# The exponentials of an attention kernel: shift read from a per-key bias instead of added by VectorE, and the range test's branch moved to the end

## The chip, the cores and the metric

The kernel runs on one core of a Trainium2 chip. The core has five engines that each run their own list of instructions in order and wait for one another through semaphores: TensorE (PE; its weight loads are shown as PEld), VectorE (DVE), ScalarE (ACT), GpSimd (POOL) and SyncE (SP, here the main issuer of DMAs). Matmul results land in PSUM, everything else is in SBUF or DRAM. The metric is device time in microseconds (us) for one execution. The kernel before takes 1242.67 us, the median of three runs (1242.14 to 1245.28).

## The reference

Two blocks, one after the other. First a causal attention whose scores get a decay bias; then a mixture of experts in which each token goes to one expert.

```python
# B, H, S, DH = 8, 8, 576, 64;  q, k = randn * 0.1;  s = randn * 0.5
scores = scale * q @ k.T                      # scale = 1/8
cum = np.cumsum(np.maximum(s, 0.0), axis=-1)
bias = -(cum[:, :, :, None] - cum[:, :, None, :])
scores = np.where(causal, -1000000000.0, scores + np.minimum(bias, 0.0))
attn = np.exp(scores - np.max(scores, axis=-1, keepdims=True))
attn = attn / (np.sum(attn, axis=-1, keepdims=True) + 1e-09)
x = attn @ v                                  # then the heads side by side: (B, S, 512)
...
logits = x @ w_gate;  local_gate = sigmoid(x @ w_local)       # 8 experts
# per batch, token after token: e = argmax(logits) at s == 0 or local_gate < 0.5,
# else the expert of the token before
out = softmax(logits)[e] * (np.maximum(x @ w1[e], 0.0) @ w2[e])   # w1: 512x1024
```

A key j after its query i is masked. For the others the bias is cum[j] - cum[i], which is never above 0, so the minimum changes nothing. Dividing by the sum takes out any factor that is the same for all keys of a query; a shift of cum by a constant is such a factor.

## The kernel before

**Stages.** attention, in_range, route, a branch, experts. `manual_schedule` means that each engine gets its instructions in the order in which the code writes them; nothing reorders them, and waits are put in where data or a buffer asks for it.

**Attention.** The 64 heads go in 32 pairs (NPAIR; HP = 4 pairs a batch, index n); the two heads of a pair lie in the two halves of the partitions of qb and kb. Scores are made key by key: the partitions are 128 keys of block c, the columns are the queries from that block on, so block 0 has 576 columns a head, then 448, 320, 192, and the last 64 keys ("tail") 64. `scores(n, c)` issues the matmuls into PSUM (L207 for block 0, L212 for blocks 1 to 3, L220 for the tail, whose 64x64 results go into free columns of the PSUM tile of block 3). VectorE then adds the bias in one pass for each head (L230, L221 for the tail): it adds cb, the cumulated sums of the queries, spread over all partitions, and subtracts ck, the value of each key, a number for each partition, and so moves the scores to SBUF. POOL masks the diagonal 128x128 squares (L232, L224), and ScalarE takes the exponential of the whole tile with both heads in SBUF (L234, L226).

`values(n, t)` multiplies with the values: query block t = 0 to 3 (L251, one matmul of 74 columns for each key block up to t and each head, with the exponentials as weights) and the tail queries (L263, and L267 for the tail keys). The 74 columns of va are the 64 of a head's v, its 9 logit columns (v times the gate weights), and a column of ones that gives the sum of the exponentials. VectorE takes reciprocals of the sums into recs (L255, L269) and scales the results (L257, L270, L271). The 9 logit columns are made once a batch by `value_logits(b)`: matmuls (L179) into PSUM, two ScalarE copies to SBUF (L181, L182), PE transposes (L185), ScalarE copies into va and vl (L187, L190).

The order within an iteration n is written in the loop at L294: scores blocks 0, 1 of pair n; values 0, 1, 2 of pair n - 1; scores blocks 2, 3 and tail of pair n; values 3 and tail of pair n - 1. After the fourth pair of a batch comes value_logits of the next one; one pair later the batch before is stored (L310, L312, the DRAM buffer x_tokens) and its logits are summed (`logits`, VectorE L280 and L283, then PE L285, into lg).

The PSUM pool ps_s has three buffers of two banks, tag "s": block 0 takes one for each head, blocks 1, 2 and 3 one for both heads, the tail shares that of block 3, and value_logits takes one for L179 and one for L185. ps_o has two buffers for values and for L285.

**Loads.** SP loads q, k, vT and v of batch b + 1 at the second pair of batch b (L118 to L123). cum is computed on VectorE before the first pair, written to DRAM, and read back spread over the partitions: cb for each pair (`load_cum`, 32 times), cbt for the tails, ctail for ck.

**After attention.** `in_range` counts on VectorE how many reciprocals in recs lie outside SUM_MIN to SUM_MAX (0.25 to 1e18), into out_of. `route` turns lg into the experts of the tokens: lists of tokens idx_g and idx_s in 43 blocks (NBLK) of 128 tokens, the expert ebi of each block and the gate. Then all engines read out_of (L76) and branch (L78): if it is over 0, attention_general computes attention again with a true maximum, and route runs again. Then `experts`, for each block: w1 and w2 of its expert are loaded by SP (L765, 2 MB each), its tokens are gathered by POOL (L773), transposed on PE (L782), two layers (L794, relu on ScalarE L795, transposes L803, L810), VectorE scales (L812), POOL scatters the rows to the output (L813).

The first weight load of the experts writes SBUF that attention and route used, so it waits for them too.

## Time and profile before

One profiled execution:

| | |
|---|---|
| profiled execution, own time | 1241.2 us |
| its span, first to last instruction | 1239.5 us |
| busy PE / PEld / DVE / ACT / POOL | 1105.6 / 653.4 / 337.4 / 198.9 / 163.6 us |
| granted TensorE clock, mean | 0.86 of full |
| attention ends (last L285) | 518.5 us |
| route and branch | 518.5 to 568.7 us |
| experts, from the first transpose of tokens | 577.8 us to the end |
| DMA | 269.44 MB, mean 217 GB/s |

How to read the rows that follow. On the page's slices the span is cut into 40 equal parts of 31 us, and a digit is the busy share of an engine there in tenths; PEclk is the TensorE clock that was granted, in tenths of full speed. In rows of groups or of the timeline, "L251 PE MATMUL po<-va,sc 128*128 128x74" is an operation of line 251 on PE that writes po from va and sc; "[1.50 <-DVE sc L230]" says that the engine stood still 1.50 us ahead of it, until the DVE operation of L230 was done. In rows of the waits, the operation that waited stands first and the one that ended the wait second. In rows of windows the start and end are followed by the length, and busy us and number of instructions of each engine, then the granted clock, the share of the 16 DMA engines and GB/s.

### The profile page before, as it was taken

Reading aid. Unit: us, or ns where it says so; the run is one execution under the profiler, and the core shown is the slowest. Engines: PE = TensorE matmul, PEld = TensorE weight load, DVE = VectorE, ACT = ScalarE, POOL = GpSimd, SP = SyncE. Lnnn points to the kernel's source line nnn. Section 1 sums busy time; section 2 is a strip of 40 time slices with the busy share of each in tenths; the row PEclk is TensorE's granted clock in tenths of the full one; section 3 lists DMA queues with packets and bytes.
Section 4 is the critical chain, followed back from the end, with each engine's and each line's share of the span. In section 5 each row is a group of like instructions: output and inputs, shape, how many; then the busy total and the mean of one; then the engine's idle time right before and its main releaser. Section 6 shows DMA issues by size and latency. Waiting matters only on the chain. (4 is left out here: it accounts for less than half of the span.)

```text
span 1239.5 us, 12883 instructions
## 1 busy us (share of the span) xinstructions
PE 1105.6 (89%) x4870; PEld 653.4 (53%) x4870; DVE 337.4 (27%) x799; ACT 198.9 (16%) x332; POOL 163.6 (13%) x306
## 2 busy tenths in 40 slices
PE   2889898989898989745999999999999999999996
PEld 1666666666576666643444445444444444444443
DVE  1544443434444444460111111111111111111110
ACT  1322222222222222100111111111111111111110
POOL 0111111111111111121011111111111111111110
PEclk9777777777767777655999999999999999999998
DMA  8616161616251611106978887878878888777860
GB/s 247 217 53 216 54 214 56 213 56 212 77 191 45 224 47 31 39 1 253 409 305 308 311 318 309 316 308 316 323 308 319 319 313 317 308 305 297 307 227 4
DMA packets 47959, 269.44 MB, mean 217 GB/s; under 512 B 18381, under 2 KB 18381, under 8 KB 33808
## 3 DMA queue, kind: packets, MB, share of 16 engines
q1 hardware_dynamic: 39920, 247.79, 54.0%
q0 software_dynamic: 6880, 20.72, 4.2%
q8 instruction: 41, 0.67, 0.2%
q10 hardware_dynamic: 1088, 0.02, 0.1%
q14 instruction: 30, 0.25, 0.1%
HBM read 249.48 MB, written 20.86 MB: 218 GB/s over the span
## 5 line engine op out<-in xcount | busy, mean ns | idle before, releaser
L794 PE MATMUL hp<-w1b,xT 128*128 128x512 f32 x688 | 311.8, 597 | 0.8 <-DVE xT L784 0.8
L810 PE MATMUL yp<-w2b,hT 128*128 128x512 f32 x688 | 302.4, 593 | 0.3 <-ACT hT L804 0.3
L810 PEld LDWEIGHTS yp<-w2b,hT 128*128 128x128 f32 x688 | 130.9, 190 | 164.3 <-issue 163.8
L794 PEld LDWEIGHTS hp<-w1b,xT 128*128 128x128 f32 x688 | 128.4, 192 | 146.0 <-issue 144.9
L251 PEld LDWEIGHTS po<-va,sc 128*128 128x128 f32 x1280 | 179.8, 226 | 36.2 <-issue 33.9
L251 PE MATMUL po<-va,sc 128*128 128x74 f32 x1280 | 191.0, 315 | 0.0
L230 DVE SCALAR_TENSOR_TENSOR sc<-cb,ck,ps 128x576 f32<-128x576 f32 (+3 forms) x256 | 141.5, 609 | 135.0 <-issue 62.7
L234 ACT ACTIVATE sc<-sc 128x1152 f32<-128x1152 f32 (+3 forms) x128 | 105.0, 843 | 299.6 <-POOL sc L232 299.1
L795 ACT ACTIVATE hs<-hp 128x512 f32<-128x512 f32 x86 | 51.4, 597 | 615.9 <-PE hp L794 615.9
L812 DVE TENSOR_SCALAR y<-yp,gate 128x512 f32<-128x512 f32 x43 | 32.3, 751 | 401.6 <-PE yp L810 401.6
L813 POOL DMA_INDIRECT out_dram<-y,idx_s x43 | 43.6, 1015 | 564.2 <-DVE y L812 564.2
L232 POOL TENSOR_SCALAR_AFFINE_SELECT sc<-sc 128x256 f32<-128x256 f32 x128 | 51.8, 406 | 422.8 <-DVE sc L230 408.5
L212 PE MATMUL ps<-qb,kb 64*128 64x320 f32 (+2 forms) x384 | 88.0, 569 | 0.0
L207 PE MATMUL ps<-qb,kb 64*128 64x512 f32 (+1 forms) x256 | 74.5, 731 | 0.0
L804 DVE COPY hT<-htp 128x512 f32<-128x512 f32 x43 | 29.7, 691 | 155.2 <-PE htp L803 151.6
L207 PEld LDWEIGHTS ps<-qb,kb 64*128 64x128 f32 x256 | 36.9, 312 | 36.8 <-issue 35.9
L220 PE MATMUL ps<-qb,kb 64*64 64x64 f32 x128 | 10.8, 246 | 48.3 <-DVE sc L230 48.3
L803 PEld LDWEIGHTS htp<-ident,hs 128*128 128x128 f32 x344 | 40.3, 141 | 22.6 <-issue 22.6
L773 POOL DMA_INDIRECT xg<-x_tokens,idx_g x43 | 42.0, 978 | 21.8 <-issue 12.8
L803 PE MATMUL htp<-ident,hs 128*128 128x128 f32 x344 | 44.6, 273 | 0.0
L212 PEld LDWEIGHTS ps<-qb,kb 64*128 64x128 f32 x384 | 39.4, 233 | 8.4 <-DVE sc L230 1.1
L263 PE MATMUL pot<-va,sc 128*64 128x74 f32 x512 | 40.1, 336 | 0.0
(129 smaller groups left out, 426.8 us busy)
## 6 DMA issues: line engine op xcount, KB each, us to landing
w1b<-in_w_dram SPq DMA_DIRECT2D x43, 2048.0 KB, 13.5
w2b<-in_w_dram SPq DMA_DIRECT2D x43, 2048.0 KB, 8.5
cb<-cum SPq DMA_DIRECT2D x32, 576.0 KB, 4.6
qb<-in_q_dram SPq DMA_DIRECT2D x8, 1152.0 KB, 6.1
kb<-in_k_dram SPq DMA_DIRECT2D x8, 1152.0 KB, 8.2
vTb<-in_vT_dram SPq DMA_DIRECT2D x8, 1152.0 KB, 10.7
va<-in_vm_dram SPq DMA_DIRECT2D x8, 1024.0 KB, 15.4
x_tokens<-xb SPq DMA_DIRECT2D x8, 1024.0 KB, 4.3
```

The costliest lines, as they stand in the source:

```text
L207: mm(ps[h][:, a:z], lhsT=kb[d, hp, :P], rhs=qb[d, hp, a:z], start=True, stop=True)
L212: mm(both[:, h, :w], lhsT=kb[d, hp, c * P : c * P + P], rhs=qb[d, hp, c * P :], start=True, stop=True)
L230: nc.vector.scalar_tensor_tensor(sc[:, h], cb[:, h, c * P :], ck[:, i : i + 1], ps[h], Alu.subtract, Alu.add)
L232: nc.gpsimd.affine_select(out=diag, in_=diag, compare_op=Alu.is_ge, fill=MASKED / scale, base=0, pattern=[[0, 2], [1, P]], channel_multipl ...
L234: nc.scalar.activation(sc, sc, Act.Exp, scale=scale)
L251: mm(po[:, t % 2, h, :], lhsT=sc[c][:, h, (t - c) * P : (t - c + 1) * P], rhs=va[:, c, 2 * hp + h, :], start=(c == 0), stop=(c == t))
L773: nc.gpsimd.indirect_dma_start(out=xg[i][:, :], out_offset=None, in_=x_d[:, :], in_offset=bass.IndirectOffsetOnAxis(ap=idx_g[:, i : i + 1] ...
L794: mm(ps, lhsT=xT[i][:, c, :], rhs=ws[i][0][:, c, f], start=(c == 0), stop=(c == DK - 1))
L795: nc.scalar.activation(hs[i][:, f], ps, Act.Relu)
L803: tr(ps[:, j, :], h[:, (g + j) * P : (g + j + 1) * P], ident)
L810: mm(ps, lhsT=h[:, c, :], rhs=ws[i][1][:, c, :], start=(c == 0), stop=(c == FK - 1))
L813: nc.gpsimd.indirect_dma_start(out=out[:, :], out_offset=bass.IndirectOffsetOnAxis(ap=idx_s[:, i : i + 1], axis=0), in_=y[:, :], element_o ...
```

## The change

The scores' pass on VectorE goes. ScalarE takes the exponential straight from PSUM, exp(scale * score + bias), where the bias is a number for each key (a partition): its cumulated sum less that of a reference token. For the query side only that reference matters, since a factor per query falls out in the division. There are two references, GROUPS and MIDS: queries 0 to 255 are shifted by the sum at token 128, queries 256 to 575 by that at token 416. The exponentials then no longer have their largest value near 1, so the bounds of in_range become 1e-20 and 1e20, and the branch that computes all again outside of them stands behind the experts, with a second call of route and experts inside it.

The bias of all keys is made once: rel (cum less the reference) is transposed on PE into PSUM (L172 and L176 of the new program) and copied to SBUF. cum doesn't go through DRAM, and cb, cbt, ctail and ck are gone. The masked squares are now set to 0 behind the exponential instead of to -1e9 ahead of it.

The scores of a pair are cut anew, in four units of one PSUM buffer each (UNITS; a piece is key block, reference group, first and last query): block 1's first 128 queries with block 0's first 256 and the tail; block 0's and block 3's remaining 320 and 192; block 1's remaining 320; block 2's 320. One exponential is issued for each piece and head, twelve a pair, and one for the tail.

value_logits' copies move from ScalarE to VectorE, and its two halves (L179 with its copies, L185 with its copies) stand behind two different pairs. Its call for batch 0 stands behind the scores of pair 0. q and k of batch 0 are asked for first, one pair at a time; q, k, vT of a next batch one iteration earlier than before, v where it was (vt in a layout that needs one DMA). attention_general and the host code change only for that layout.

```diff
-SUM_MIN, SUM_MAX = 0.25, 1e18
+SUM_MIN, SUM_MAX = 1e-20, 1e20
+GROUPS = ((0, 2 * P), (2 * P, S))
+MIDS = (P, 13 * TL // 2)
+UNITS = (
+    ((1, 0, P, 2 * P), (0, 0, 0, 2 * P)),
+    ((0, 1, 2 * P, S), (3, 1, 3 * P, S)),
+    ((1, 1, 2 * P, S),),
+    ((2, 1, 2 * P, S),),
+)
...
+    experts(tc, w1, w2, out, x_d, ident, ebi, idx_g, idx_s, gate)
     wrong = nc.values_load(out_of[0:1, 0:1], min_val=0, max_val=P * NPAIR * (2 * NF + 1),
                            skip_runtime_bounds_check_because="a count of elements")
     with tc.If(wrong > 0):
         attention_general(tc, q, k, vm, vt, s, w_gate, w_local, cum_d, x_d, ident, lg)
         route(tc, ident, lg, ebi, idx_g, idx_s, gate)
-    experts(tc, w1, w2, out, x_d, ident, ebi, idx_g, idx_s, gate)
+        experts(tc, w1, w2, out, x_d, ident, ebi, idx_g, idx_s, gate)
...
+        for p in parts:
+            nc.sync.dma_start(qb[:, p], q[b][:, p])
+            nc.sync.dma_start(kb[:, p], k[b][:, p])
...
+    def load_v(b):
+        if b < B:
+            nc.sync.dma_start(vas[b % 2][:, :, :, :DH], vm[b])
+            nc.sync.dma_start(vls[b % 2][:, :, :DH], vt[b])
...
+    load_qk(0, [slice(i, i + 1) for i in range(HP)])
...
+    bps = ps_s.tile([P, 2, 512], F32, name="bps", tag="s")[:, 0]
+    bias_of, at = {}, 0
+    for g, (q0, q1) in enumerate(GROUPS):
+        rel = once.tile([BH, q1], F32, name=f"rel{g}")
+        nc.vector.tensor_scalar(rel, cum[:, :q1], cum[:, MIDS[g] : MIDS[g] + 1], None, Alu.subtract)
+        for c in range(min(NF, q1 // P)):
+            tr(bps[:, at : at + BH], rel[:, c * P : (c + 1) * P], ident[:BH, :BH])
+            bias_of[g, c] = at
+            at += BH
+    for h in range(2):
+        mm(bps[h * TL : h * TL + TL, at : at + NPAIR], lhsT=rel[:, TS:],
+           rhs=ident[:BH, :BH].rearrange("k (n h) -> k h n", h=2)[:, h], start=True, stop=True)
+    bias_of["tail"] = at
+    bias = once.tile([P, at + NPAIR], F32, name="bias")
+    nc.vector.tensor_copy(bias, bps[:, : at + NPAIR])
...
+        if step == 0:
+            vTb = vTs.pop(b)
+            ps = ps_s.tile([P, 2, 512], F32, name="vwp", tag="s").rearrange("p a c -> p (a c)")
+            for a, z in ((0, 512), (512, S)):
+                for hp in range(HP):
+                    mm(ps[hp * 32 : hp * 32 + 32, a:z], lhsT=wbd[:, hp, :], rhs=vTb[:, hp, a:z], start=True, stop=True)
+            vw = vls_of[b] = p_sm.tile([P, NB * P], F32, name="vw")
+            nc.vector.tensor_copy(vw[:, :S], ps[:, :S])
+            nc.vector.tensor_copy(vw[:, S:], ps[:, TS:S])
+            return
+        vw = vls_of.pop(b)
+        pt = ps_s.tile([P, 2, 512], F32, name="vwt", tag="s").rearrange("p a c -> p (a c)")
...
+    def scores(n, u):
         b, hp = divmod(n, HP)
         qb, kb = ins[b]
         heads = [slice(DH * h, DH * h + DH) for h in range(2)]
+        tail = u == 0
+        ps = ps_s.tile([P, 2, 512], F32, name="ps", tag="s")
+        w = sum(q1 - q0 for _, _, q0, q1 in UNITS[u])
+        sc = scs[n, u] = p_sc.tile([P, 2, w], F32, name=f"sc{u}")
+        at, places = 0, []
+        for c, g, q0, q1 in UNITS[u]:
             for h, d in enumerate(heads):
+                mm(ps[:, h, at : at + q1 - q0], lhsT=kb[d, hp, c * P : c * P + P], rhs=qb[d, hp, q0:q1],
+                   start=True, stop=True)
+            places.append((c, g, q0, at, at + q1 - q0))
+            at += q1 - q0
+        if tail:
+            for d in heads:
+                mm(ps[d, 0, at : at + TL], lhsT=kb[d, hp, TS:], rhs=qb[d, hp, TS:], start=True, stop=True)
+        diag = []
+        for c, g, q0, a, z in places:
+            for h in range(2):
+                i = bias_of[g, c] + 2 * n + h
+                nc.scalar.activation(sc[:, h, a:z], ps[:, h, a:z], Act.Exp, bias=bias[:, i : i + 1], scale=scale)
+            if q0 == c * P:
+                diag.append(a)
+        if diag:
+            step = diag[1] - diag[0] if len(diag) > 1 else P
+            x = sc[:, :, diag[0] : diag[0] + step * len(diag)].rearrange("p h (n c) -> p h n c", c=step)[:, :, :, :P]
+            nc.gpsimd.affine_select(out=x, in_=x, compare_op=Alu.is_ge, fill=0.0, base=0,
+                                    pattern=[[0, 2], [0, len(diag)], [1, P]], channel_multiplier=-1)
+        if tail:
+            sct = scs[n, "t"] = p_sc.tile([P, TL], F32, name="sct")
+            i = bias_of["tail"] + n
+            nc.scalar.activation(sct, ps[:, 0, at : at + TL], Act.Exp, bias=bias[:, i : i + 1], scale=scale)
+            for d in heads:
+                nc.gpsimd.affine_select(out=sct[d], in_=sct[d], compare_op=Alu.is_ge, fill=0.0, base=0,
                                         pattern=[[1, TL]], channel_multiplier=-1)
+    def weights(n, c, t, h):
+        for u, pieces in enumerate(UNITS):
+            at = 0
+            for cc, g, q0, q1 in pieces:
+                if cc == c and q0 <= t * P < q1:
+                    a = at + t * P - q0
+                    return scs[n, u][:, h, a : a + min(P, S - t * P)]
+                at += q1 - q0
...
+                    mm(po[:, t % 2, h, :], lhsT=weights(n, c, t, h), rhs=va[:, c, 2 * hp + h, :],
+                       start=(c == 0), stop=(c == t))
...
-    value_logits(0)
     for n in range(NPAIR + 1):
         b, hp = divmod(n, HP)
+        if hp == 0 and n:
+            load_qk(b + 1, [slice(0, HP)])
         if hp == 1:
-            load_batch(b + 1)
-        load_cum(n + 2)
-        for what, us in ((scores, (0, 1)), (values, (0, 1, 2)), (scores, (2, 3, 4)), (values, (3, 4))):
+            if b == 0:
+                load_qk(1, [slice(0, HP)])
+            load_v(b + 1)
+        for what, us in ((scores, (0, 1)), (values, (0, 1, 2)), (scores, (2, 3)), (values, (3, 4))):
             for u in us:
                 if what is scores and n < NPAIR:
                     scores(n, u)
                 if what is values and n:
                     values(n - 1, u)
-        if hp == HP - 1:
-            value_logits(b + 1)
+        if n == 0:
+            value_logits(0, 0)
+            value_logits(0, 1)
+        if hp >= 2:
+            value_logits(b + 1, hp - 2)
```

What becomes of the engines' lists, between scores and values. PE before, from the end of values 2 of a pair (sc_235 to sc_238 are the exponentials of blocks 0 to 3 of the pair before):

```order
L212 MATMUL ps<-qb,kb 128x320 [waits DVE_49]
L212 MATMUL ps<-qb,kb 128x320
L212 MATMUL ps<-qb,kb 128x192 [waits DVE_49]
L212 MATMUL ps<-qb,kb 128x192
L220 MATMUL ps<-qb,kb 64x64 [waits DVE_49]
L220 MATMUL ps<-qb,kb 64x64
L251 MATMUL po<-va_99,sc_235 128x74
L251 MATMUL po<-va_99,sc_236 128x74
```

and after (sc_217, sc_234, sc_266, sc_272 are those of the four units of the pair before; the two score lines are now L220 and, for the tail, L226, the values L271 and L283):

```order
L220 MATMUL ps<-qb,kb 128x128 [waits Activation_49]
L220 MATMUL ps<-qb,kb 128x128
L220 MATMUL ps<-qb,kb 128x256 x2
L226 MATMUL ps<-qb,kb 64x64 x2
L220 MATMUL ps<-qb,kb 128x320 [waits Activation_49]
L220 MATMUL ps<-qb,kb 128x320
L220 MATMUL ps<-qb,kb 128x192 x2
L271 MATMUL po<-va_108,sc_217 128x74 [waits DVE_49,PE_49,Pool_49]
L271 MATMUL po<-va_108,sc_217 128x74 x5
L271 MATMUL po<-va_108,sc_234 128x74 [waits DVE_49,PE_49]
L271 MATMUL po<-va_108,sc_266 128x74
L271 MATMUL po<-va_108,sc_272 128x74 [waits Pool_49]
```

The tail's matmuls, which stood behind a second use of block 3's buffer with a wait for DVE of their own, are in the first unit; the waits of score matmuls on DVE have become waits on ScalarE, and that of the values on POOL is new.

DVE before, one pair:

```order
L230 SCALAR_TENSOR_TENSOR sc_337<-cb,ck,ps 128x576 x2
L230 SCALAR_TENSOR_TENSOR sc_338<-cb,ck,ps 128x448 x2
L255 RECIPROCAL recs<-po 128x4
L257 TENSOR_TENSOR xb<-po,recs 128x2x128
L257 TENSOR_TENSOR lb<-po,recs 128x2x18
L230 SCALAR_TENSOR_TENSOR sc_339<-cb,ck,ps 128x320 x2
L230 SCALAR_TENSOR_TENSOR sc_340<-cb,ck,ps 128x192 x2
L221 SCALAR_TENSOR_TENSOR sct<-cbt,ck,ps 128x64
```

and after:

```order
L275 RECIPROCAL recs<-po 128x4
L277 TENSOR_TENSOR xb<-po,recs 128x2x128
L277 TENSOR_TENSOR lb<-po,recs 128x2x18
L289 RECIPROCAL recs<-pot 128x1
L290 TENSOR_SCALAR xl<-pot,recs 128x64
L291 TENSOR_SCALAR ll<-pot,recs 128x9
```

The score passes (L230, L221) are gone and the reciprocals and scalings are all that is left, but for the copies of value_logits (L194 to L205).

ScalarE before, one pair:

```order
L234 ACTIVATE sc_235<-sc_235 128x1152
L234 ACTIVATE sc_236<-sc_236 128x896
L234 ACTIVATE sc_237<-sc_237 128x640
L234 ACTIVATE sc_238<-sc_238 128x384
L226 ACTIVATE sct<-sct 128x64
```

and after, one pair:

```order
L231 ACTIVATE sc_217<-ps,bias 128x128 x2
L231 ACTIVATE sc_217<-ps,bias 128x256 x2
L242 ACTIVATE sct<-ps,bias 128x64
L231 ACTIVATE sc_234<-ps,bias 128x320 x2
L231 ACTIVATE sc_234<-ps,bias 128x192 x2
L231 ACTIVATE sc_266<-ps,bias 128x320 x2
L231 ACTIVATE sc_272<-ps,bias 128x320 x2
```

Five exponentials over SBUF have become thirteen out of PSUM with half or less of the columns each.

SP around the first weight load, before (the first row is the branch that leaves the body of the condition; L760 reads the block's expert):

```order
L78 UNCONDITIONAL_BRANCH
L78 UNCONDITIONAL_BRANCH [waits DMAHW0_49,DMAHW1_49,DMAHW2_49,DMAHW3_49,DMAHW4_49,DMAHW5_49,DMAHW6_49,DMAHW7_49]
L760 TENSOR_LOAD ebi [waits DVE_49]
L765 ISA
L765 DMA w1b<-in_w_dram 128x4096 [waits DMAHW2_49,DMAHW1_49,DMAHW3_49,DVE_49,DMAHW5_49,PE_49,DMAHW6_49,Activation_49,Pool_49]
L765 ISA
L765 DMA w2b<-in_w_dram 128x4096 [waits DMAHW4_49,DMAHW5_49,DMAHW3_49,DMAHW7_49,DMAHW2_49,DMAHW0_49]
```

and after, directly behind the last store of attention:

```order
L336 DMA x_tokens<-xl 256x1x64 [waits DMAHW1_49,DVE_49]
L336 DMA x_tokens<-xl 256x1x64 [waits DMAHW2_49]
L785 TENSOR_LOAD ebi [waits DVE_49]
L790 ISA
L790 DMA w1b<-in_w_dram 128x4096 [waits PE_49,DMAHW3_49,Activation_49,Pool_49]
L790 ISA
L790 DMA w2b<-in_w_dram 128x4096 [waits DMAHW4_49]
```

The branch is gone from this place; it now stands behind the last block's loads, and on the other engines behind their last instruction of the experts.

116 lines of the change are left out of this document (22 added, 94 removed).

## The prediction

> **What bounds the kernel now.** I read the page's slices first, then the waits of the attention stage, then its windows cut at the clock's own steps. The page:
>
> ```profile
> span 1239.5 us, 12883 instructions
> PE   2889898989898989745999999999999999999996
> PEclk9777777777767777655999999999999999999998
> ```
>
> Two stages are TensorE's: attention (slices 1 to 16) and the experts from 578 us on. In the experts PE is full at full clock, and the change leaves them alone. In attention PE is busy too, but at 0.7 of the clock. The stage ends here:
>
> ```profile
> 518.15 0.35 PE L285 MATMUL ltp<-lt,fold 128*64 128x9 f32 x2 [1.53 <-DVE lt L283]
> ```
>
> The waits from 60 to 500 us (waiter, what it waited for, us in total, times, longest):
>
> ```profile
> PE ps L220 <- DVE sc L230: 41.8, 28, 1.5
> PE ltp L285 <- DVE lt L283: 10.7, 7, 1.5
> ```
>
> Once a pair PE stands for 1.5 us at the tail scores until VectorE's score pass frees a PSUM buffer. 1.5 us of a 14 us pair would be little, but see the windows of 3.41 us (columns: length, busy us of PE, PEld, DVE, ACT, POOL, then PEclk):
>
> ```profile
> 198.95:202.36 3.41, 3.41 (x15) 2.05 (x15) 0.08 (x1) 0.67 (x3) 0.00 (x0) 0.50 0.00 0
> 202.36:205.78 3.42, 3.42 (x28) 2.77 (x26) 3.26 (x7) 1.34 (x2) 0.81 (x2) 1.00 0.00 0
> 205.78:209.19 3.41, 1.91 (x17) 1.32 (x17) 1.85 (x5) 1.53 (x3) 0.81 (x2) 1.00 0.00 0
> 209.19:212.60 3.41, 3.41 (x23) 3.27 (x24) 0.43 (x3) 0.67 (x2) 0.47 (x2) 0.50 0.02 5
> 212.60:216.02 3.42, 1.89 (x22) 1.52 (x20) 1.79 (x8) 0.00 (x0) 0.00 (x0) 0.50 0.66 246
> 216.02:219.43 3.41, 3.41 (x12) 1.21 (x10) 1.33 (x2) 0.00 (x0) 0.00 (x0) 0.50 0.97 242
> 219.43:222.84 3.41, 3.41 (x30) 3.18 (x30) 2.19 (x6) 2.11 (x2) 0.81 (x2) 1.00 0.98 408
> ...
> 506.15:509.56 3.41, 3.41 (x18) 3.38 (x17) 1.06 (x5) 0.00 (x0) 0.00 (x0) 0.50 0.00 0
> ```
>
> The clock is 1.00 or 0.50 for whole windows. It falls after the window that holds the stall (PE 1.91 of 3.41 us), stays up through a full window of value matmuls (202.36), and rises only after a full window rich in score matmuls (198.95, 216.02: PEld 2.05 and 1.21), not after a full one of values, which is mostly weight loading (209.19, 506.15: 3.27 and 3.38). So the stall costs 1.5 us and then some 7 us at half speed, pair after pair. That is what bounds the stage.
>
> The Trainium skill (TensorE: Matmul & The Clock Gate, Part 1) lets the clock fall only after at least one idle window of about 3.4 us; the rows above differ, since 1.5 us of idle is enough. By that page the stall is not the cause of the half clock, which is the second rival below.
>
> **The sum.** At full clock the pieces of a pair show once without a break, and the rest at half clock:
>
> ```profile
> 322.27 0.76 PE L185 MATMUL vwt<-ident,vw 128*128 128x128 f32 x5 [0.76 <-ACT vw L181]
> 322.96 1.30 PE L207 MATMUL ps<-qb,kb 64*128 64x512 f32 x8
> 324.10 0.97 PE L212 MATMUL ps<-qb,kb 64*128 64x448 f32 x4
> 325.00 2.90 PE L251 MATMUL po<-va,sc 128*128 128x74 f32 x24
> 327.83 1.14 PE L212 MATMUL ps<-qb,kb 64*128 64x320 f32 x8
> 330.47 0.33 PE L220 MATMUL ps<-qb,kb 64*64 64x64 f32 x4 [1.50 <-DVE sc L230]
> 330.73 2.50 PE L251 MATMUL po<-va,sc 128*128 128x74 f32 x16
> ...
> 70.47 1.25 PE L263 MATMUL pot<-va,sc 128*64 128x74 f32 x16
> 71.66 0.51 PE L267 MATMUL pot<-vl,sct 64*64 64x74 f32 x4
> 72.10 2.15 PE L179 MATMUL vwp<-vTb,wbd 128*32 128x512 f32 x16
> 75.00 1.33 PE L185 MATMUL vwt<-ident,vw 128*128 128x128 f32 x5 [0.76 <-ACT vw L181]
> ```
>
> Values of a pair, counted from start to start: t = 0, 1, 2 in 2.83 us; t = 3 is 16 such records, two thirds, 1.89; the tail rows at half clock are 1.19 + 0.44, halved 0.81. Together 5.53 us. Scores: 1.14 + 0.90 + 0.98 (1.14 less the 0.16 that such rows overlap) = 3.02 us for 1536 columns a head. The new units have the same 1536 columns in six pieces for five; one more set of weights is about 0.15 us (the 0.98 us for two pieces hold some 0.1 to 0.2 beyond the columns' rate in the first row); the tail 0.26. So 3.43 us. A pair then takes 8.96 us where it took 14.
>
> From the first value matmul to the end: 32 x 5.53 = 177; 31 further score sets x 3.43 = 106; seven value_logits at (2.15/2 + 0.69) = 12; eight batch ends, whose wait on L283 stays, at 1.53 + 0.3 = 15. Sum 310 us at full clock. The eight waits of 1.53 us are as long as the stall removed, so each may drop the clock when it falls inside one window. I take five falls, each two or three windows at half (6.8 to 10.2 us, so 3.4 to 5.1 lost), 21 us; bounds 0 and some 50 (all eight, and slower rises). So 331 us.
>
> **Start.** The value matmuls start at 34.74 us now, late because cum goes through DRAM and back before pair 0. Windows of the start (last two columns: DMA share, GB/s) and that first row:
>
> ```profile
> 6.00:8.00 2.00, 0.43 (x4) 0.24 (x3) 0.00 (x0) 0.00 (x0) 0.00 (x0) 1.00 1.01 412
> 16.00:18.00 2.00, 0.00 (x0) 0.00 (x0) 0.00 (x0) 0.00 (x0) 0.00 (x0) 1.00 1.20 180
> 18.00:20.00 2.00, 0.00 (x0) 0.00 (x0) 0.00 (x0) 0.00 (x0) 0.00 (x0) 1.00 0.11 33
> 34.74 1.45 PE L251 MATMUL po<-va,sc 128*128 128x74 f32 x11
> ```
>
> Batch 0 and the gate weights are in by 18 us, and the change moves the same bytes, q and k first. Now the order is scores of pair 0 (from some 8 us, as q, k and the bias come), then vwp at about 18, when the gate weights are in: 2.15 + 0.76 (the wait for the copy) + 1.33 (vwt at half clock), then two units of pair 1 in 1.9 (full) to 3.8 us (half), and the values: 24 us (22 to 27). So attention ends at 24 + 331 = 355 us for 518.5: 163 us gained.
>
> **What is taken off VectorE and put on ScalarE.**
>
> ```profile
> L230 DVE SCALAR_TENSOR_TENSOR sc<-cb,ck,ps 128x576 f32<-128x576 f32 (+3 forms) x256 | 141.5, 609 | 135.0 <-issue 62.7
> L795 ACT ACTIVATE hs<-hp 128x512 f32<-128x512 f32 x86 | 51.4, 597 | 615.9 <-PE hp L794 615.9
> L226 ACT ACTIVATE sct<-sct 128x64 f32<-128x64 f32 x32 | 8.2, 256 | 8.7 <-POOL sct L224 8.6
> L182 ACT COPY vw<-vwp 128x64 f32<-128x64 f32 x8 | 1.7, 218 | 0.0
> ```
>
> VectorE loses 141.5 us, all beside PE but for the stall; the moved copies of value_logits give it 1.6 us a batch, under matmuls. ScalarE has 13 exps a pair from PSUM with a bias read from SBUF, 3136 columns in all; no row has both. Low end, PSUM reads without the bias: 218 ns for 64 and 597 for 512 columns are 0.164 us + 0.85 ns a column, so 13 x 0.164 + 3136 x 0.85 = 4.8 us. High end, VectorE's pass, from PSUM with a scalar for each partition: 609 ns for a mean of 384 columns; 13 x 0.21 + 3136 x 1.04 = 6.0 us. I take 5.3, by L226, the nearest exp. All of this is under 8.96 us, so it hides beside PE. What is late next is a PSUM buffer: the fourth unit needs the first unit's, whose five exps (2 us) have 0.95 (second unit) + 2.83 (three values) + 0.65 (third unit) = 4.4 us from its last matmul.
>
> The Trainium skill (ScalarE: Activation LUTs, What ACT_TABLE_LOAD costs) gives 280 ns + 0.833 ns a column where the bias is a pointer operand; an estimate by it is 13 x 0.28 + 3136 x 0.000833 = 6.3 us a pair, and the sum would be the same, as this also hides. No row here has the case.
>
> The selects now follow the exps (three and two small ones, some 2 us a pair on POOL) and are read by the value matmuls of the next iteration, several us later: nothing. On SP the 32 cb loads go; q, k and vT are asked for ahead of the token store of the batch before, which nothing waits for until the gathers: nothing. vwt no longer waits for its copy, since it stands a pair later.
>
> **The branch.** Around the branch, and the last store of now:
>
> ```profile
> 564.16 0.20 DVE L735 SCALAR_TENSOR_TENSOR idx_s<-id,empty 128x43 int32<-128x43 f32 x1
> 568.67 0.37 SPq L765 DMA_DIRECT2D w1b<-in_w_dram  x1
> 568.83 1.16 POOL L773 DMA_INDIRECT xg<-x_tokens,idx_g  x1 [9.02 <-DVEq L78]
> 577.78 1.09 PE L782 MATMUL xp<-ident,xg 128*128 128x128 f32 x4 [14.20 <-DMA xg<-x_tokens,idx_g]
> ...
> 1230.54 0.98 POOL L813 DMA_INDIRECT out_dram<-y,idx_s  x1 [7.31 <-DVE y L812]
> ```
>
> The weight load and the gather stand 4.5 us behind idx_s for the branch. Without it the gather goes at once: 4.4 us gained (0 if the weights, asked for earlier, slow the gather; 9 at most, all of what it took). At the end the same branch stands behind the last store: 0 if it runs while the store lands (the span ends 8 us after L813), 4.5 if not; I take 3.
>
> Sum: 1241.2 - 163 - 4.4 + 3 = 1077 us, against the profiled execution's 1241.2 us (span 1239.5), 0.1% under the median of 1242.67.
>
> **The rivals.**
> A. The clock goes on alternating within pairs, because the low value windows or the batch ends pull it down as often as now. Then only waiting is saved: L220's 48.3 us, the start's 10.7, the branch's 1.4: 1181 us. For it: five falls are my guess, and half clock once held for a whole stretch.
>
> ```profile
> L220 PE MATMUL ps<-qb,kb 64*64 64x64 f32 x128 | 10.8, 246 | 48.3 <-DVE sc L230 48.3
> 340.60 5.40 PE L251 MATMUL po<-va,sc 128*128 128x74 f32 x24
> ```
>
> Against: no fall in the rows shown came without a stalled window. By the skill's page above it would be this case.
> B. ScalarE becomes the bound. That takes a mean of 8.96 / 13 = 0.69 us an exp, beyond the 0.6 us of a 512-column row; at 0.9 us, 11.7 us a pair, 32 x 2.7 = 88 us come back: 1165 us.
> C, on the other side: the clock does not rise. Here it needs a full window of scores, and the change cuts them into smaller pieces, with more weight loads (16 records for 12 in the first two units) and the tail between. If no window lifts it, the stage runs at half: 5.40 for 2.90 us is 1.86, so 24 + 1.86 x 310 = 601 us, total 1322. It decides where a window at half clock has more weight loading than the 2.05 of 3.41 us that still lifted it; the new stretch comes to about that share, but scores of two units still last 3.9 us, more than a window.
> D. The branch is taken and all is computed again: over 1000 us more. Worked out from the inputs, the sums lie between 1e-17 and 7e18, inside 1e-20 to 1e20.
>
> **How the numbers follow.** Forecast 0.70, A 0.14, B 0.08, C 0.06, D 0.02. The forecast's own range is 1050 (no falls, start at 22) to 1115 (50 us lost to the clock, late start). For 8 in 10 I go from 1045 up to 1170, which takes in B and half of A, and leaves out C, D and the rest. 0.3% (4 us) is about what can be told from no change; only C and D are slower, and between the cases nothing lies near 1242: faster 0.91, same 0.01, slower 0.08.
>
> **What would show it.** PEclk 1.00 in most attention windows, with falls only behind L304's wait (L285 now); a pair in about 9 us; no wait of PE on ScalarE above some 0.2 us; first value matmul at 24; ScalarE busy 5 to 6 us a pair; xp some 9 us after idx_g. A clock row still changing twice a pair is A; PE waiting for the exps is B; a clock row of 0.5 through attention is C.

## The result, and the profile after

The changed kernel takes 1087.56 us, the median of four runs (1069.00 to 1093.37), against 1243.97 for the kernel before (four runs, 1242.14 to 1247.43). The ratio is 0.8646, 95% interval 0.8546 to 0.8746; it leaves out runs more than 1.5% above the fastest, and the two traces of this kernel below, 27.1 us apart, differ by how often and how long the clock fell. The profiled execution, at 1093.37 us, is the longest of the four; its parts are set against 1241.2 us below.

From the page, to be held against the same rows of before:

```profile
span 1091.7 us, 12831 instructions
PE   4999999999999646999999999999999999999994
PEclk7899978899898855999999999999999999999997
```

Attention now ends in slice 14 instead of 17, and its clock row reads 8 or 9 in most slices where it read 7. The last row of the stage, and all that PE waited for between 60 and 350 us (waiter, releaser, us, times, longest):

```profile
371.67 0.25 PE L304 MATMUL ltp<-lt,fold 128*64 128x9 f32 x2 [1.51 <-DVE lt L302]
PE ltp L304 <- DVE lt L302: 10.5, 7, 1.5
```

The wait of the tail scores is gone without a successor. What is left are the seven waits of 1.5 us at the batch ends inside the stage. Windows cut at the clock's steps around one of them, and around the two that cost nothing (length, busy us of PE, PEld, DVE, ACT, POOL, then PEclk):

```profile
145.39:148.80 3.41, 3.41 (x28) 2.75 (x28) 0.53 (x2) 1.79 (x6) 0.42 (x1) 1.00 0.71 300
148.80:152.21 3.41, 1.90 (x30) 1.62 (x29) 1.99 (x8) 0.30 (x1) 0.42 (x1) 1.00 0.27 102
152.21:155.63 3.42, 3.42 (x20) 2.24 (x22) 0.16 (x1) 1.10 (x4) 0.00 (x0) 0.50 1.04 274
...
165.87:169.28 3.41, 3.41 (x30) 3.06 (x29) 0.71 (x3) 0.00 (x0) 0.00 (x0) 0.50 0.00 0
169.28:172.69 3.41, 3.41 (x22) 2.17 (x20) 0.59 (x3) 1.16 (x4) 0.00 (x0) 0.50 0.00 0
172.69:176.11 3.42, 3.42 (x32) 3.12 (x30) 0.71 (x3) 1.96 (x6) 1.48 (x4) 1.00 0.00 0
...
107.84:111.25 3.41, 2.56 (x35) 2.25 (x34) 1.47 (x7) 1.04 (x3) 0.42 (x1) 1.00 0.07 27
111.25:114.67 3.42, 2.76 (x26) 1.99 (x26) 0.67 (x3) 1.28 (x5) 0.00 (x0) 1.00 1.07 332
...
244.37:247.79 3.42, 1.91 (x30) 1.40 (x30) 2.15 (x9) 0.00 (x0) 0.00 (x0) 1.00 0.54 202
247.79:251.20 3.41, 3.41 (x32) 2.92 (x31) 0.41 (x2) 2.93 (x9) 1.06 (x3) 1.00 1.02 251
```

At 148.80 the whole wait lies in one window (PE 1.90 of 3.41 us) and the clock is half for the next six; at 107.84 the step between two windows cuts the wait in two (2.56 and 2.76) and the clock stays. At 244.37 the whole wait lies in one window (1.91) and the clock stays all the same. Five of the seven batch ends cost a fall in this trace, with 16 windows at half clock behind them: 16 x 3.41 / 2 = 27 us.

The windows of the whole stage, from the first value matmul to the last matmul of the batch ends (L304; L285 before), for this kernel and those of the experiments:

| kernel | stage from | length, us | PE busy, us | mean clock |
|---|---|---|---|---|
| before | 34.74 | 483.41 | 419.67 | 0.72 |
| after, first trace | 28.81 | 342.86 | 330.81 | 0.91 |
| after, second trace | 25.78 | 318.77 | 306.73 | 0.98 |
| after, matmul of the batch ends deferred (defer) | 28.11 | 303.24 | 301.74 | 1.00 |
| before, tail scores ahead (tail_ahead) | 33.88 | 337.77 | 320.19 | 0.93 |
| the same, and batch ends deferred (two_waits) | 33.88 | 314.27 | 303.96 | 0.99 |
| after, tail scores behind the exponentials of their unit (tail_late) | 29.92 | 501.08 | 443.62 | 0.68 |
| defer, 0.9 us of wait a pair (wait_0.9) | 28.49 | 376.78 | 347.58 | 0.87 |
| defer, 0.65 us of wait a pair (wait_0.5) | 28.35 | 318.91 | 297.81 | 1.00 |

So the 147.8 us between the two profiled executions are 140.6 in the stage, 5.9 at the start, and 1.3 behind it.

### The profile page after: what moved, and what is told of

The parts are those of the page before. It is cut to its first block, busy times and chain, and to the rows that moved or that the text cites. A ratio compares the mean times of both kernels' runs of the same rounds, so it can differ in the third digit from the quotient of the medians.

```text
span 1091.7 us, 12831 instructions
## 1 busy us (share of the span) xinstructions
PE 1019.5 (93%) x5003; PEld 611.5 (56%) x5003; DVE 201.9 (18%) x553; ACT 228.9 (21%) x548; POOL 157.7 (14%) x274
## 4 chain that ended last, share of the span: by engine, by line
PE 93%; DVE 3%; DMA 2%; POOL 0%; issue 0%; SPq 0%; ACT 0%; POOLq 0%; DVEq 0%; ACTq 0%
PE hp L819 27%; PE yp L835 27%; PE po L271 15%; PE ps L220 10%; PE htp L828 3%; PE pot L283 2%; PE xp L807 2%; PE table L752 2%; DMA wbd<-in_w_local_dram 1%; PE vwp L192 1%; PE pot L287 1%; PE ps L226 1%; DMA xg<-x_tokens,idx_g 1%; PE vwt L200 1%; DMA qb<-in_q_dram 1%; DVE lg L299 0%
## 5 line engine op out<-in xcount | busy, mean ns | idle before, releaser
L231 ACT ACTIVATE sc<-ps,bias 128x320 f32<-128x320 f32 (+3 forms) x384 | 151.4, 485 | 197.2 <-PE ps L226 126.4
L271 PEld LDWEIGHTS po<-va,sc 128*128 128x128 f32 x1280 | 162.6, 208 | 23.7 <-issue 23.6
L271 PE MATMUL po<-va,sc 128*128 128x74 f32 x1280 | 172.1, 295 | 0.0
L220 PE MATMUL ps<-qb,kb 64*128 64x320 f32 (+3 forms) x768 | 125.1, 450 | 0.6 <-ACT sct L242 0.6
L838 POOL DMA_INDIRECT out_dram<-y,idx_s x43 | 43.6, 1015 | 563.1 <-DVE y L837 563.1
L237 POOL TENSOR_SCALAR_AFFINE_SELECT sc<-sc 128x256 f32<-128x256 f32 (+1 forms) x96 | 47.3, 493 | 298.8 <-ACT sc L231 298.8
L220 PEld LDWEIGHTS ps<-qb,kb 64*128 64x128 f32 x768 | 68.9, 210 | 22.1 <-issue 6.3
L275 DVE RECIPROCAL recs<-po 128x4 f32<-128x4 f32 x64 | 11.7, 183 | 245.7 <-PE po L271 245.7
L807 PE MATMUL xp<-ident,xg 128*128 128x128 f32 x172 | 26.3, 276 | 9.0 <-DMA xg<-x_tokens,idx_g 9.0
L809 DVE COPY xT<-xp 128x512 f32<-128x512 f32 x43 | 29.3, 680 | 15.6 <-PE xp L807 15.6
L752 PE MATMUL table<-val,place 128*128 128x86 f32 x80 | 17.8, 424 | 12.7 <-POOL val L750 12.7
L277 DVE TENSOR_TENSOR xb<-po,recs 128x256 f32<-128x256 f32 x64 | 27.2, 424 | 2.2
```

Source lines behind the costliest of these rows:

```text
L220: mm(ps[:, h, at : at + q1 - q0], lhsT=kb[d, hp, c * P : c * P + P], rhs=qb[d, hp, q0:q1], start=True, stop=True)
L231: nc.scalar.activation(sc[:, h, a:z], ps[:, h, a:z], Act.Exp, bias=bias[:, i : i + 1], scale=scale)
L237: nc.gpsimd.affine_select(out=x, in_=x, compare_op=Alu.is_ge, fill=0.0, base=0, pattern=[[0, 2], [0, len(diag)], [1, P]], channel_multipli ...
L271: mm(po[:, t % 2, h, :], lhsT=weights(n, c, t, h), rhs=va[:, c, 2 * hp + h, :], start=(c == 0), stop=(c == t))
L752: mm(table.rearrange("p k b -> p (k b)"), lhsT=place[:, m - c0, :], rhs=val[:, m].rearrange("p k b -> p (k b)"), start=(m == 0), stop=(m = ...
L807: tr(ps[:, c, :], x[:, c * P : (c + 1) * P], ident)
```

## The experiments

All times are medians. The kernel before took 1240 to 1243 us beside each of them (single runs 1219.89 to 1245.99).

**The changed kernel again.** 

> The changed kernel once more, for a second trace. Theory: the clock falls in the window of 3.41 us that holds the wait of a batch end (1.51 us, PE ltp L304 <- DVE lt L302), and only where most of the wait lies inside one window; since the windows run freely, which of the eight batch ends cost something changes from run to run. So the time lies between 1065 and 1095 us, the falls stand at batch ends and at the start alone, but not at the same batch ends as in the first trace (there: 5 of 7, and 16 windows at half clock behind them, 16 x 3.41 / 2 = 27 us). Rival: the falls belong to what the batch holds (loads, value_logits); then the same batch ends fall again and the time is that of the first trace.

Measured: 1081.70 us (1066.29 to 1093.16, six runs). The second trace, at 1066.29 us:

```profile
PEclk8999999999999558999999999999999999999997
```

Three batch ends cost a fall, the 2nd, 4th and 6th (near 101, 183 and 265 us), and each was over after one window at half clock; in the first trace it was the 1st, 3rd, 4th, 6th and 7th, and 16 windows. So two of the three are the same as before, but the sets differ, and the rival, that the falls belong to particular batches, does not hold. The two traces differ by 24.1 us in the stage and by 27.1 as a whole. Cut at the clock's steps, 9 of the 14 waits lie whole in one window (PE 1.90 to 1.92 us) and 8 of these cost a fall; the 5 that a step cuts (2.23 to 2.56 in the emptier window) cost none. The spread of this kernel comes from this and from how soon a later window lifts the clock again.

**The batch ends' matmul deferred.**

```diff
-    def logits(b):
+    def sum_logits(b):
...
+    def fold_logits(b):
+        lt, m0 = xs.pop((b, "sum")), b * NB
         ps = ps_o.tile([TL, E + 1], F32, name="ltp", tag="o")
         mm(ps, lhsT=fold, rhs=lt, start=True, stop=True)
...
+            if what is values and us[0] == 0 and hp == 1 and b:
+                fold_logits(b - 1)
...
-            logits(b - 1)
+            sum_logits(b - 1)
+            if n == NPAIR:
+                fold_logits(b - 1)
```

> The changed kernel, with the small matmul of a batch end (L304) put behind the first values of the second pair of the next batch, so that PE has no wait there. Theory (a wait of 1.5 us inside one clock window drops the clock): seven waits of 1.51 us go (10.6 us), and all falls between the start and the end of attention go with them, 27 us in the first trace; attention ends at 372 - 38 = 334 us, the run takes about 1055 us against that trace's 1093, and the repeats lie within a few us of each other. Rival A (windows rich in value matmuls pull the clock down by themselves, the wait only decides where): only the 10.6 us go, about 1082 us, clock still changing, repeats as far apart as before.

Measured: 1053.35 us (1052.94 to 1053.78, five runs), ratio to before 0.8488 (0.8447 to 0.8529). Of its page, and one pair of its timeline, which has no wait in it:

```profile
PEclk8999999999997559999999999999999999999997
212.13 2.90 PE L271 MATMUL po<-va,sc 128*128 128x74 f32 x24
214.96 1.35 PE L220 MATMUL ps<-qb,kb 64*128 64x320 f32 x8
216.24 2.01 PE L271 MATMUL po<-va,sc 128*128 128x74 f32 x16
218.18 0.73 PE L283 MATMUL pot<-va,sc 128*64 128x74 f32 x16
218.84 0.35 PE L287 MATMUL pot<-vl,sct 64*64 64x74 f32 x4
219.12 0.93 PE L220 MATMUL ps<-qb,kb 64*128 64x128 f32 x8
219.97 0.33 PE L226 MATMUL ps<-qb,kb 64*64 64x64 f32 x4
220.23 1.13 PE L220 MATMUL ps<-qb,kb 64*128 64x320 f32 x8
221.30 0.89 PE L271 MATMUL po<-va,sc 128*128 128x74 f32 x6
```

The last batch end, behind which no pair follows, keeps its wait. There is no fall between the start and the end of the stage, the spread went from 27 to 0.8 us, and the time is the theory's 1055, within 2 us. Rival A, that value-rich windows pull the clock down by themselves, is ruled out: this stage has the same values.

**Before, with the tail scores ahead of the pass.** Two lines move (a third, which sets a, is repeated), VectorE's pass stays.

```diff
             if c == NF - 1:
                 scs[n, "t"] = both
+                a = TL + P
+                for h, d in enumerate(heads):
+                    mm(both[d, 0, a : a + TL], lhsT=kb[d, hp, TS:], rhs=qb[d, hp, TS:], start=True, stop=True)
...
-            for h, d in enumerate(heads):
-                mm(both[d, 0, a : a + TL], lhsT=kb[d, hp, TS:], rhs=qb[d, hp, TS:], start=True, stop=True)
```

> The kernel before, with one thing changed: the 64x64 tail scores (L220) are issued straight behind the matmuls of block 3, ahead of VectorE's pass over that block, so that they no longer wait for it (48.3 us in all, 1.5 a pair). VectorE's score pass, cb, the exponentials in SBUF, the branch and the start all stay. Theory (the wait drops the clock, not the pass itself): VectorE has 215 us of work in attention, 6.7 us a pair, which still hides beside a pair of about 9 us at full clock, so most of what the whole change gained comes from here: 1100 to 1170 us, the higher the more often block 0, which takes two of the three PSUM buffers, now waits for VectorE in its turn. Rival (the wait costs its own time and no more): 1243 - 48 = 1195 us with the clock row of before. Rival (VectorE's pass is the bound): no gain, the wait goes to other scores, about 1240 us.

Measured: 1089.59 us (1077.41 to 1096.50), ratio 0.8714 (0.8648 to 0.8781). Its clock row, and the waits of PE between 40 and 365 us:

```profile
PEclk9988999996999855999999999999999999999998
PE ltp L286 <- DVE lt L284: 10.7, 7, 1.5
PE vwt L185 <- ACT vw L181: 5.3, 7, 0.8
```

The wait for L230 of 48.3 us is gone and nothing took its place, though VectorE still does all its passes. This is the time of the whole change, to what the two can be told apart, and lower than the theory's 1100 to 1170, which had counted on new waits for VectorE. The wait was the cause of the fallen clock; the time that the pass takes on VectorE was not.

**After, with the tail scores behind the four exponentials of their unit.**

```diff
-        if tail:
-            for d in heads:
-                mm(ps[d, 0, at : at + TL], lhsT=kb[d, hp, TS:], rhs=qb[d, hp, TS:], start=True, stop=True)
         diag = []
...
         if tail:
+            for d in heads:
+                mm(ps[d, 0, at : at + TL], lhsT=kb[d, hp, TS:], rhs=qb[d, hp, TS:], start=True, stop=True)
             sct = scs[n, "t"] = p_sc.tile([P, TL], F32, name="sct")
```

> The changed kernel, with the tail's 64x64 scores issued behind the four exponentials of their unit instead of ahead of them, so that PE waits once a pair as it did before, now for ScalarE: four exponentials of 0.36 to 0.48 us, about 1.5 us a pair, 48 us in all. Everything else is as in the changed kernel. Theory (1.5 us of waiting a pair drops the clock): the clock alternates again as in the kernel before (0.73 in attention), a pair takes some 13 to 14 us and attention ends near 29 + 32 x 13.5 = 460 us, total 1170 to 1220 us. Rival (the wait costs its own time): 1087 + 48 = 1135 us.

Measured: 1247.11 us (1211.61 to 1267.46). Its clock row and the same waits (40 to 525 us):

```profile
PEclk8565957567978665855999999999999999999998
PE ps L238 <- ACT sc L228: 45.4, 30, 1.5
PE ltp L303 <- DVE lt L301: 10.5, 7, 1.5
```

The same 1.5 us a pair, now made by ScalarE, takes back all that the change had gained. The median is above the theory's 1170 to 1220, and only the shortest run lies inside: attention ends at 531 us for the theory's 460, and the stage's mean clock is 0.68, under the 0.72 of before. In this trace the clock fell less often but stayed down longer: without falls that the start or the end of the stage cuts, 14 falls with 86 windows at half clock, up to 16 in a row, against 29 with 76, at most 8 in a row, in the kernel before. That the smaller score pieces lift a fallen clock less often, the thought behind the prediction's rival C, would fit; no run took it apart.

**Before without both waits.** 

> The kernel before with both waits taken away and nothing else: the tail scores issued ahead of VectorE's pass over block 3, and the small matmul of a batch end put behind the first values of the second pair of the next batch. VectorE's score pass, the exponentials in SBUF, the loads and the branch stay. Theory (the two waits and the clock are the whole gain; moving the pass to ScalarE is worth nothing by itself): the run with only the first edit took 1090 us; from it go 7 x 1.53 = 11 us and its 13 to 14 windows at half clock between 70 and 300 us, 23 us: 1052 to 1065 us, within 10 us of the changed kernel with the same second edit (1053). Rival (a kernel that has VectorE's pass cannot stay at full clock, since its score blocks wait for it elsewhere): 1080 to 1095 us, clock still changing.

Measured: 1070.97 us (1066.58 to 1073.28), ratio 0.8633 (0.8573 to 0.8693): above the theory's range and under the rival's. Waits of PE between 40 and 345 us:

```profile
PE vwt L185 <- ACT vw L181: 5.3, 7, 0.8
PE ps L212 <- DVE sc L231: 3.5, 5, 1.4
```

With the clock up, VectorE is late at times after all (L212, 3.5 us; behind the longest of these waits, 1.4 us, the clock falls once, for two windows), and PE stands for the copies of value_logits. By the two traces, 17.4 us lie between this kernel and defer: 11.0 in the stage, 5.8 at the start (33.88 against 28.11), 0.6 behind it. This is what the rest of the change is worth together. In the stage it is these two waits (8.8 us) and up to 3.4 for the fall; of the waits only the one on L231 belongs to VectorE's pass, and the other to value_logits, which the change also splits. The start was 5.8 us later with cum's way through DRAM and the old load order. The removed waits on VectorE's pass and at the batch ends, with the clock, are worth the rest.

**How long a wait it takes.** Both on top of defer: the tail's scores behind the first piece of the second unit, and behind the whole second unit; the tail's exponential and mask go with them. The first run has

```diff
+            if u == 1 and n in tails:
+                tail_scores(n)
```

inside the loop over the pieces, and the second, behind it,

```diff
+        if u == 1:
+            tail_scores(n)
```

> The changed kernel with the deferred matmul of the batch ends (1053.4 us), and the tail's scores issued behind the first two matmuls of the second unit, with the tail's exponential behind that; they wait for the four exponentials of their unit, of which some 0.6 us are covered by these matmuls, so that PE stands still some 0.9 us a pair instead of the 1.5 of the run with the tail behind its exponentials (1247 us). Theory with a threshold (windows of which PE is busy for three quarters, 2.56 of 3.41 us, kept the clock in the trace of the changed kernel, those with 1.91 lost it): the clock stays at 1.00, only the waits are paid: 1053 + 32 x 0.9 = 1082 us. Rival (every wait of PE costs the clock in proportion to its length): six tenths of the 194 us between 1053 and 1247, some 1170 us.

> As the run with a wait of 0.9 us a pair (1120 us), with the tail's scores one score block later, behind the whole second unit, so that about 0.3 us more of the exponentials is covered and PE waits some 0.5 to 0.6 us a pair. In the trace with 0.9 us the clock fell in windows with PE busy 2.42 us and PEld 1.9 to 2.1 (values around the wait), and stayed up in windows with the same 2.42 us of PE and PEld 1.6 (scores around the wait). Theory (what counts is how much matmul work a window holds, not whether PE waits): with 0.3 us more work in such a window none falls, and only the waits are paid: 1053 + 32 x 0.55 = 1071 us. Rival (any wait every pair brings some falls, in proportion): 39 us of clock at 0.9 us of wait, so some 24 at 0.55, 1095 us.

Measured: 1120.17 us (1113.01 to 1126.94) and 1069.15 us (1068.70 to 1070.28). The waits of the first, and two of its windows:

```profile
PE ps L216 <- ACT sc L248: 28.1, 31, 1.0
161.12:164.54 3.42, 2.44 (x25) 2.13 (x23) 0.03 (x1) 2.72 (x8) 1.11 (x3) 1.00 0.99 292
202.08:205.50 3.42, 2.44 (x23) 1.65 (x24) 1.27 (x6) 1.36 (x5) 0.45 (x1) 1.00 1.01 422
```

and the waits of the second:

```profile
PE ps L216 <- ACT sc L248: 19.6, 30, 0.7
```

At 0.65 us a pair (19.6 / 30) only the waits are paid: 32 x 0.65 = 21 us of them, of which 15.8 show in the time, since a little else goes on meanwhile; the stage's clock is 1.00, and the theory's 1071 holds. At 0.9 us the expectation of 1082 failed: 29 us of waits and some 38 of clock. Both windows shown have the same wait and the same 2.44 us of PE; the clock fell behind the first, which has more weight loading (2.13 us, value matmuls around the wait), and stayed up behind the second (1.65, scores around it). So neither the length of the wait nor the busy time of PE decides alone. Weight loading does not either: in the second trace of the changed kernel this window, with the same PE and PEld as the one that fell, kept the clock:

```profile
223.75:227.16 3.41, 2.44 (x34) 2.13 (x33) 1.59 (x7) 0.92 (x3) 0.42 (x1) 1.00 0.12 48
```

A count of matmul work orders the windows better. Count for each matmul record the columns that it streams, times the share of the 128x128 array that it uses: 74 for a value record `128*128 128x74`, 160 for a score record `64*128 64x320`, and split a record that crosses a step by its time. By this count the windows of the changed kernel's two traces that hold a batch end's wait, or the larger part of it, lost the clock at 1100 to 1352 and kept it at 1355 (the one at 244.37, just past the highest that fell) to 1635. Over the windows of the stage in all the table's traces and in that of gates_first, none at full clock under 1350 kept it and none over 1600 lost it; none at half clock under 1410 lifted it and none over 1660 failed to. In between both happened, and no run set the count by itself, so what the clock goes by stays open.

**The start.** Both on top of defer: gate weights asked for first, on POOL's queue instead of ScalarE's; then value_logits(0) behind the first two units of pair 1.

```diff
+    for h in range(2):
+        for w, a, z in ((w_gate, 0, E), (w_local, E, E + 1)):
+            nc.gpsimd.dma_start(wbd[h * DH : h * DH + DH, :, h * WR + a : h * WR + z],
+                                w.rearrange("(a h d) e -> h d a e", h=2, d=DH)[h])
     load_qk(0, [slice(i, i + 1) for i in range(HP)])
...
-            nc.scalar.dma_start(wbd[h * DH : h * DH + DH, :, h * WR + a : h * WR + z],
-                                w.rearrange("(a h d) e -> h d a e", h=2, d=DH)[h])
```

> The changed kernel with the deferred matmul of the batch ends (1053.4 us), and the gate weights (wbd) asked for ahead of q and k, on POOL's queue. In that run PE stands still from 13.8 us until wbd is in at 20.5 us, the clock falls and stays at half until 27 us. Theory: with wbd there at about 8 us PE goes from the scores of pair 0 straight to vwp, no window is empty, values start at 19 to 22 us instead of 28.8 and at full clock: 8 to 12 us less, 1042 to 1046 us. Rival (vT or v, not wbd, sets the start): 0 to 3 us less.

> The run with the gate weights asked for first (1049.3 us), with value_logits of batch 0 written behind the first two score units of pair 1 instead of behind the scores of pair 0. In that trace PE waits 1.55 us for vT and 0.96 us for a copy, the clock falls at 16.7 us and is half until 26.9. Theory: the units of pair 1 fill the wait for vT; no window has too little work, the clock stays up, values start some 2 us earlier: 1041 to 1046 us. Rival (the units wait for ScalarE's exponentials of pair 0, which end at 14.9 us, so vwp only comes later and the clock falls all the same): 1048 to 1052 us.

Measured: 1049.27 us (1048.88 to 1051.46) and 1050.01 us (1047.98 to 1057.22). First the rows of defer, then those of the run with the gate weights first:

```profile
20.39 2.15 PE L192 MATMUL vwp<-vTb,wbd 128*32 128x512 f32 x16 [6.29 <-DMA wbd<-in_w_local_dram]
28.11 2.90 PE L271 MATMUL po<-va,sc 128*128 128x74 f32 x24
```

```profile
15.07 1.18 PE L192 MATMUL vwp<-vTb,wbd 128*32 128x512 f32 x16 [1.55 <-DMA vTb<-in_vT_dram]
22.43 5.40 PE L271 MATMUL po<-va,sc 128*128 128x74 f32 x24
```

Values start 5.7 us earlier, but at half clock (5.40 us for what takes 2.90): the clock falls at 16.7 us, behind a window that holds the wait for vT and half of the one for the copy (PE 1.39 of 3.41 us). The stage takes 306.93 us for defer's 303.24, so attention ends 2.0 us earlier in these traces. By the medians the gain is 4 us instead of 8 to 12, a little above the rival's 0 to 3. With the other order, values wait 1.55 us for v in turn, and nothing is gained that these runs can tell, which is the rival's range. Gates first has the lowest median of all versions: 0.8463 of before (0.8410 to 0.8516).

**The route stage.** On top of defer: spare matmuls whose result nobody reads, ahead of the table's; then the same with five buffers for place and blk and with the start's order.

```diff
+    for _ in range(13):
+        mm(pos, lhsT=ones, rhs=flat, start=True, stop=True)
```

> The changed kernel with the deferred matmul of the batch ends (1053.4 us), and 13 matmuls of 320 columns whose result nobody reads, in the route stage behind pos and ahead of the table's matmuls, where PE waits 12.6 us for POOL at half clock. Theory (a full window of matmuls lifts the clock): the spare ones take 0.7 us each at half clock and 0.35 at full, the clock rises after at most two windows, and the 80 table matmuls then take about 9 us instead of 17.75; 6 to 9 us less, 1044 to 1047 us. Rival (VectorE and POOL set the pace of the table, 1.7 and 1.5 us a step): 0 to 3 us less.

> The run above with the route stage changed as well: 13 spare matmuls ahead of the table's, as in the run that had these alone (no gain there: the table's matmuls then waited 4.1 us for POOL and VectorE, which waited for PE to free place and blk, and the clock fell again), now with five buffers each for place and blk instead of two, so that VectorE never waits for PE. Theory: table's matmuls at full clock, paced by VectorE (1.73 us a step): idx_s some 6 us earlier, 1036 to 1041 us. Rival (the table's waits for the first steps still drop the clock): no more than 2 us below the run above.

Measured: 1053.58 us (1052.81 to 1055.34) and 1051.58 us (1045.72 to 1053.34): no gain in either over the runs that they were put on (1053.35 and 1050.01). The table's matmuls of the first:

```profile
362.76 3.80 PE L762 MATMUL table<-val,place 128*128 128x86 f32 x32 [1.60 <-POOL val L760]
369.07 9.55 PE L762 MATMUL table<-val,place 128*128 128x86 f32 x48 [2.50 <-POOL val L760]
```

The clock did rise: 32 matmuls took 3.80 us, where at half clock all 80 took 17.75. Then PE was ahead of POOL, stood for 2.50 us, and the clock was half again for the rest. A faster PE behind a slower feeder makes its own wait.

**The branch back between route and experts**, on top of defer. 

> The changed kernel with the deferred matmul of the batch ends (1053.4 us, repeats within 0.8), and the branch put back between route and the experts, where it stood before. From the first traces: without the branch the first transpose of tokens came 8.37 us behind idx_s instead of 13.62 (5.25 us less), and the span ended 13.35 us behind the last store's issue instead of 8.97 (4.38 us more). Theory (the branch costs nearly the same at both places): 1053.4 + 0.9 = 1054 us. Rival (the forecast's lower bound, the branch at the end is covered by the last store's landing, so moving it gained all it cost): 1057 to 1059 us.

Measured: 1053.64 us (1052.60 to 1054.69), 0.3 us beside defer: moving the branch is worth nothing that these runs can tell. The traces of the two kernels, which differ in nothing else, show why: with the branch in the middle the first transpose comes 13.10 us behind idx_s, without it 8.45, and the span goes on 8.9 us behind the last store's issue for 13.35. So it costs 4.65 us in the middle and 4.4 at the end.

## Why the prediction was right, and where its sizes were off

It said 1077 (1045 to 1170); 1087.56 came, and the likeliest case is the one that happened. That the number is so near is in part luck: single runs of this kernel lie between 1066 and 1093 us, by a chance that the prediction had put in as a mean. (Its remark on the Trainium skill's page TensorE: Matmul & The Clock Gate, Part 1, speaks of "the second rival"; it means rival A.)

- **The cause.** "The stall costs 1.5 us and then some 7 us at half speed": shown from both sides. Taking the wait out of the old kernel gives the gain, putting it into the new one takes it back. Rival A is ruled out by defer. PE was busy 1.90 us in a window behind which the clock fell, and 2.44 in another; the rule of the Trainium skill (TensorE: Matmul & The Clock Gate, Part 1) that the prediction cited, a fall after an idle window, differs from these rows. "Each may drop the clock when it falls inside one window" holds as a chance: 8 of 9 such waits did. Rivals C and D did not come in: the clock rises, though once only after six windows, and no second attention runs.
- **The full-clock sum**, 310 us with eight batch ends. In defer it can be read alone: 303.24 us with one such wait; with the other seven (10.6) it would be 314, so the sum was 4 short. A pair takes 221.30 - 212.13 = 9.17 us for 8.96: values 2.83 + 1.94 + 0.94 = 5.71 for 5.53, scores 1.28 + 2.18 = 3.46 for 3.43. The halved tail rows were the weak part (0.94 for 0.81). Over 32 pairs that is 6.7 us; the other terms were too high by some 3.
- **Falls at the batch ends**, five with 21 us: 27 us in the first trace, some 5 in the second (three windows). The bounds 0 and 50 were needed; a single number for something that is settled by where a clock window happens to lie is a mean over chances.
- **The start**, 24 us (22 to 27): 28.81 and 25.78. The term that was off is "at about 18, when the gate weights are in": in the second trace vwp started at 17.45, but in the first it waited until 20.48, and the values started outside the bounds. In the first trace the nearly empty windows before it (0.81 and then 0.00 us of PE) dropped the clock for the start's own matmuls.
- **ScalarE**, 5.3 us a pair. By form:

```profile
L231 ACT ACTIVATE sc<-ps,bias 128x320 f32<-128x320 f32 x192 | 88.4, 536 | 70.8 <-PE ps L220 70.2
L231 ACT ACTIVATE sc<-ps,bias 128x256 f32<-128x256 f32 x64 | 26.8, 478 | 0.0
L231 ACT ACTIVATE sc<-ps,bias 128x192 f32<-128x192 f32 x64 | 24.5, 458 | 0.0
L231 ACT ACTIVATE sc<-ps,bias 128x128 f32<-128x128 f32 x64 | 20.0, 363 | 126.4 <-PE ps L226 126.4
L242 ACT ACTIVATE sct<-ps,bias 128x64 f32<-128x64 f32 x32 | 10.6, 331 | 0.0
```

  Busy 170.3 us / 32 = 5.3 a pair, under 9.17, and PE waits for the exponentials once, 0.6 us, in the whole run: rival B is out. A single one takes 331 ns for 64 columns and 536 for 320, 280 ns + 0.80 ns a column, and the three forms between lie within 25 ns of this line. The durations of a pair's thirteen add up to 6.15 us; they are busy for 5.3 since they overlap, by 0.83 / 13, some 64 ns each. The line agrees with the rule of the Trainium skill (ScalarE: Activation LUTs, What ACT_TABLE_LOAD costs) that the prediction cited. The prediction's estimate by it, 6.3 us, left out what the same section adds, that back-to-back ones overlap by some 93 ns.
- **The branch.** Rows of the changed kernel, for those of the prediction:

```profile
417.58 0.20 DVE L760 SCALAR_TENSOR_TENSOR idx_s<-id,empty 128x43 int32<-128x43 f32 x1
425.95 1.08 PE L807 MATMUL xp<-ident,xg 128*128 128x128 f32 x4 [8.95 <-DMA xg<-x_tokens,idx_g]
1078.35 0.98 POOL L838 DMA_INDIRECT out_dram<-y,idx_s  x1 [7.31 <-DVE y L837]
```

  Without it the first transpose comes 8.37 us behind idx_s instead of 13.62, 5.25 gained for the 4.4 forecast. At the end the span goes on 13.35 us behind the last L838 instead of 8.97, 4.38 lost for the 3 taken, close to the upper bound: the last store's landing does not hide it. Net 0.9 for 1.4 across these two kernels, and nothing that can be told in the run that put it back.

The sum: attention ends at 371.67 in the first trace for 355, of which 4.8 are the start, 4 the full-clock sum, and the remaining 8 the clock: the falls, and the first 7 us of the stage, which ran at half.

## What to carry to other kernels

Where TensorE carries a stage and its clock row alternates, price a wait by the clock window that it empties, not by its length: here 1.5 us a pair cost (1242.88 - 1089.59) / 32 = 4.8, and 0.65 us no more than itself. Before a rewrite that takes work off another engine, look whether the one wait it removes can be removed by itself; two moved lines gave as much here as the whole change. Look at the spread of the runs as well: 27 us of it came from seven waits of 1.5 us, and moving one small matmul took away the waits and the spread.

## What the runs showed of the hardware

- A wait of 1.5 us that lay whole inside one clock window of 3.41 us was followed by a fall in 8 of 9 cases in the two traces of the changed kernel and in all 29 in the kernel before (PE 1.90 to 1.92 us). In tail_late, among other matmuls, windows with PE 1.90 to 1.96 us lost the clock 10 times and kept it 4 times. At 0.9 us some windows fell and some did not with the same 2.44 us of PE, and at 0.65 us none fell within the stage.
- Back to full clock is not a matter of being busy: in the first trace PE was busy for six whole windows in a row at half clock (152.21 to 172.69), and the clock rose only behind the last. Weight loading doesn't settle it: 2.24 us did not lift the clock at 152.21, and the same 2.24 did at 70.29.
- A branch of all engines that is not taken cost 4.65 us in the middle and 4.4 at the end (branch_back against defer).
